# Folding the even columns of a 1024-point transform a third time, both ways, with the spectra kept by column mod 4

## The chip, the cores and the metric

The kernel runs on one core of one Trainium2 chip. The metric is the device time of one execution in microseconds (us); lower is better. Before the change it was 1444.42 us, the median of 3 runs (1443.12 to 1444.52). In this kernel TensorE does the 7562 matmuls (1394.8 us busy) and writes them to the memory PSUM; VectorE (674.9 us) and ScalarE (420.0 us) do most of the rest, among it the evictions, the copies out of PSUM. The granted clock is the share of TensorE's full speed that the profile records. The profile's span is some 2 us shorter than the device time of the same execution (1438.6 against 1440.49 us in before).

## The reference

A gated mix of two branches over x (2048 x 1024), forward and backward. Branch A is a 2-D real FFT, a product with a complex weight and the inverse FFT; branch B is a two-layer MLP with squared ReLU. Cut to what matters:

```python
def _A_ref(x, w_r, w_i):                       # B, S, D = 1, 2048, 1024
    X = jnp.fft.rfft2(x.astype(jnp.float32), axes=(-2, -1))
    X = X * (w_r + 1j * w_i)
    return jnp.fft.irfft2(X, s=(S, D), axes=(-2, -1)).astype(jnp.bfloat16)

def _B_ref(x, w1, b1, w2, b2):                 # F = 3584
    h = jnp.einsum("bsd,df->bsf", x, w1) + b1
    r = jnp.where(h > 0, h, 0)
    return jnp.einsum("bsf,fd->bsd", r * r, w2) + b2

g = sigmoid((x * gate_w).sum(-1, keepdims=True))
out = g * _A_ref(...) + (1 - g) * _B_ref(...)
_out, _vjp = jax.vjp(_f, A_x, A_w_r, A_w_i, B_w1, B_b1, B_w2, B_b2, gate_w)
_grads = _vjp(grad_out)                        # nine outputs in all
```

## The kernel before

The 2-D transform is done twice in parallel (T = 0 for x, T = 1 for the output gradient). In the first stage each of 2 x 16 row tiles goes through `one_s1`. VectorE folds the 1024 columns: `uv` is the sum and difference of the two halves (sum: even columns of the transform, difference: odd), `f` folds each once more about its middle. TensorE then does a small transform along the rows (`pk`) and the **column stage** (`pu`): eight matmuls of 2305 columns in all, 1281 of them for the even columns. P = 128, Q = 256, H = 512, D = 1024.

```python
    def one_s1(fb, cf, T, i, xt, kmat):
        uv = fb.tile([P, 2, H], FDT, name="uv", tag="uv", bufs=2)
        V(out=uv[:, 0, :], in0=xt[:, 0:H], in1=xt[:, H:D], op=ALU.add)
        V(out=uv[:, 1, :], in0=xt[:, 0:H], in1=xt[:, H:D], op=ALU.subtract)
        f = fb.tile([P, 4, Q], FDT, name="f", tag="f", bufs=2)
        a0, a1 = uv[:, :, 1:Q], uv[:, :, H - 1 : Q : -1]
        V(out=f[:, 0:2, 1:Q], in0=a0, in1=a1, op=ALU.add)
        V(out=f[:, 2:4, 1:Q], in0=a0, in1=a1, op=ALU.subtract)
        # (cut: two copies of single elements)
        pk = fps.tile([P, 8, P], FP32, name="pk", tag="ps2", bufs=2)
        fl = f[:].rearrange("p a b -> p (a b)")
        for b in range(8):
            mm(pk[:, b, :], lhsT=fl[:, b * P : (b + 1) * P], rhs=kmat, start=True, stop=True)
        ft = fb.tile([P, 8, P], FDT, name="ft", tag="ft", bufs=2)
        nc.scalar.copy(out=ft[:], in_=pk[:])
        pu = fps.tile([P, 2, H], FP32, name="pu", tag="ps2", bufs=2)
        column_stage(FWD, pu, ft, cf)
        u = fb.tile([P, H, 2], FDT, name="u", tag="u", bufs=2)
        nc.any.tensor_copy(out=u[:].rearrange("p j b -> p b j"), in_=pu[:])
        st(out=z_scr[T][:].rearrange("c (p i) l -> i (c p) l", i=S2)[i], in_=u[:].rearrange("p j b -> p (j b)"))

    FWD = (    # block of ft, PSUM bank, first column, columns, 1 = start + 2 = stop
        (4, 0, 0, H, 1), (0, 0, 0, Q + 1, 0), (1, 0, 0, Q + 1, 0), (5, 0, Q + 1, Q - 1, 2),
        (6, 1, 0, Q, 1), (7, 1, 0, Q, 2), (2, 1, Q, Q, 1), (3, 1, Q, Q, 2),
    )
    INV = (
        (2, 0, 0, H, 1), (0, 0, 0, Q + 1, 0), (1, 0, 0, Q + 1, 0), (3, 0, Q + 1, Q - 1, 2),
        (4, 1, 0, Q, 1), (5, 1, 0, Q, 2), (6, 1, Q, Q, 1), (7, 1, Q, Q, 2),
    )

    def column_stage(table, pu, ft, mat):
        o = 0
        for (b, bank, lo, n, f_) in table:
            mm(
                pu[:, bank, lo : lo + n], lhsT=ft[:, b, :], rhs=mat[:, o : o + n],
                start=bool(f_ & 1), stop=bool(f_ & 2), skip_group_check=True,
            )
            o += n
```

The first stage shares TensorE with the MLP's forward and first backward matmuls (`ph`, `pd`). The middle stage reads the spectra back, transforms along the rows (`px`, evicted as `x`), multiplies by the weights and goes back (`pv`); it runs beside the weight gradients (`pw`, evicted as `wo`). The inverse mirrors the first stage: `pki`, `rt`, a column stage `pui`, an eviction `e`, and folds on VectorE. Parts of the three:

```python
        # spectrum(), the eviction of the row transform; j in 0, 1
            (nc.scalar.copy if j == 0 else nc.vector.tensor_copy)(out=x[:, j, :, 0:H], in_=px[:])

        # fft_out(), one tile
                for b in range(8):
                    par, q4 = divmod(b, 4)
                    mm(pk[:, b, :], lhsT=r[:, q4 * P : (q4 + 1) * P, par], rhs=ki[:], start=True, stop=True)
                rt = fb.tile([P, 8, P], FDT, name="rt", tag="rt", bufs=2)
                nc.scalar.copy(out=rt[:], in_=pk[:])
                pu = fps.tile([P, 2, H], FP32, name="pui", tag="ps2", bufs=2)
                column_stage(INV, pu, rt, ci)
                e = fb.tile([P, 2, H], FDT, name="e", tag="e", bufs=2)
                nc.scalar.copy(out=e[:], in_=pu[:])
                tt = fb.tile([P, 2, 2, Q], FDT, name="tt", tag="tt", bufs=2)
                V(out=tt[:, 0].rearrange("p a b -> p (a b)"), in0=e[:, 0, :], in1=e[:, 1, :], op=ALU.add)
                V(out=tt[:, 1].rearrange("p a b -> p (a b)"), in0=e[:, 0, :], in1=e[:, 1, :], op=ALU.subtract)

        # mlp_grads(), the weight gradients, one block
                    wo = wb.tile([P, D], BF16, name="wo2", tag="wo2", bufs=2)
                    for hf in range(NH):
                        pw = mps.tile([P, H], FP32, name="pw", tag="pw", bufs=2)
                        # (cut: 16 matmuls)
                        last = nc.scalar.copy(out=wo[:, hf * H : (hf + 1) * H], in_=pw[:])
                    # (cut: wo is stored)
```

The opening transposes x and the scaled gradient `dbn` on TensorE (`pt`) and evicts them as `xT` (ScalarE) and `dbT` (VectorE). The order in which these streams are interleaved is written out:

```python
            for i in range(i0, i0 + 4):        # in rows()
                go = f1.tile([P, D], BF16, name="go", tag="go", bufs=4)
                ld(out=go[:], in_=go_perm[i])
                nc.vector.tensor_scalar(out=dbn[:, i, :], in0=go[:], scalar1=omg[:, i : i + 1], scalar2=None, op0=ALU.mult)
                turned(dbT, dbn[:, i, :], i, nc.vector.tensor_copy)

    row_gen, units, first = rows(), mlp_in(), first_stage()
    next(row_gen)
    for i0 in range(0, NT, 4):
        next(units), next(units)
        next(row_gen)
        next(units), next(units)
        next(row_gen, None)
    n = 0
    mixed = spread(units, first, 0.4)          # 0.4 tiles of first for each unit
    while n < 82:
        next(mixed)
        n += 1
    for _ in first:
        pass
```

## Time and profile before

| | before |
|---|---|
| device time, median of 3 runs | 1444.42 us |
| profiled execution | 1440.49 us, span 1438.6 us, mean granted clock 0.995 |
| opening: to the start of the last dbT copy | 88.5 us |
| forward stage: from there to the last dhT eviction | 439.3 us |
| middle stage: from there to the 83rd wo eviction | 355.9 us |
| inverse stage: from there to the first gxo eviction | 357.7 us |
| tail | 197.2 us |

The marks in the table are the starts of single instructions in the trace. What the change also touches are these evictions, from the groups with shapes kept apart (line, engine, operation, out<-in, shapes, count, then busy us and mean ns of one, then idle time before them):

```profile
L251 ACT CAST u<-pu 128x1024 f16<-128x1024 f32 x32 | 41.7, 1304 | 36.8 <-PE pu L267 36.8
...
L306 ACT CAST x<-px 128x1024 f16<-128x1024 f32 x16 | 16.2, 1014 | 5.9 <-PE px L305 5.9
...
L306 DVE CAST x<-px 128x1024 f16<-128x1024 f32 x16 | 19.6, 1224 | 111.5 <-PE px L305 111.5
```

The same 1024 elements take ScalarE 1304 ns into `u`, whose 16-bit elements were written at a step of two, and 1014 ns into `x`, written in runs.

### The profile page before, as it was taken

The numbers are of one execution on the slowest core, as the hardware profiler recorded it, in microseconds if no ns is written. First come the engines' busy times: TensorE is split into PE (matmuls) and PEld (weight loads), VectorE is DVE, ScalarE is ACT, GpSimd is POOL, SyncE is SP. The second block draws the span as 40 slices with busy tenths as digits, with TensorE's granted clock in tenths as the row PEclk, the third lists the DMA queues.
The fourth block names the chain that finished last, engine by engine and source line by source line (L and its number), as shares of the span: only waits on it lengthen the run. The fifth ranks groups of instructions, "written<-read, shape, count | busy, mean of one in ns | idle before, by whom it ended". The sixth has DMA issues, their size and how long they took to land. (4 is left out here: it accounts for less than half of the span.)

```text
span 1438.6 us, 19451 instructions
## 1 busy us (share of the span) xinstructions
PE 1394.8 (97%) x7562; PEld 674.0 (47%) x7562; DVE 674.9 (47%) x1303; ACT 420.0 (29%) x590; POOL 299.3 (21%) x483
## 2 busy tenths in 40 slices
PE   6689999999999999999999999999999999999997
PEld 4455555555554444444444444445554444444443
DVE  2564554455444466445554534113566555652222
ACT  4245555555553322222232222334322100000000
POOL 0012222222223333333442122111110000000000
PEclk9899999999999999999999999999999999999999
DMA  7476766666669967998977678777557647563530
GB/s 234 128 235 205 218 193 204 223 216 205 191 183 255 257 200 201 187 229 189 220 146 187 143 132 188 221 205 231 194 198 228 210 147 221 177 187 96 146 95 22
DMA packets 220214, 271.57 MB, mean 189 GB/s; under 512 B 16077, under 2 KB 153307, under 8 KB 220123
## 3 DMA queue, kind: packets, MB, share of 16 engines
q1 hardware_dynamic: 184122, 151.80, 39.9%
q0 software_dynamic: 36000, 118.54, 27.9%
q8 instruction: 59, 0.97, 0.3%
q14 instruction: 33, 0.26, 0.1%
HBM read 151.77 MB, written 118.51 MB: 188 GB/s over the span
## 5 line engine op out<-in xcount | busy, mean ns | idle before, releaser
L583 PE MATMUL ph<-xT,w1g 128*128 128x512 bf16 x896 | 218.6, 382 | 1.4 <-ACT xT L493 0.9
L591 PE MATMUL pd<-dbT,w2T 128*128 128x512 bf16 x896 | 215.3, 383 | 1.6 <-DVE dbT L493 1.6
L692 PE MATMUL pw<-grp,res 128*128 128x512 bf16 x896 | 209.6, 387 | 0.0
L675 PE MATMUL pw<-dbn,grp 128*128 128x512 bf16 x896 | 198.0, 379 | 1.5 <-DVE row L639 1.5
L753 PE MATMUL acc<-w,hblk 128*128 128x512 bf16 x896 | 198.6, 379 | 0.0
L794 PE MATMUL accg<-w1Tr,hblk 128*128 128x512 bf16 x896 | 193.5, 379 | 0.0
L591 PEld LDWEIGHTS <-w2T 128*128 128x128 bf16 x896 | 87.4, 99 | 109.1 <-issue 5.1
L585 ACT ACTIVATE rT<-ph,b1col 128x512 bf16<-128x512 f32 x112 | 77.0, 688 | 207.9 <-PE ph L583 159.7
L794 PEld LDWEIGHTS <-hblk 128*128 128x128 bf16 x896 | 87.7, 98 | 105.7
L675 PEld LDWEIGHTS <-grp 128*128 128x128 bf16 x896 | 87.1, 98 | 105.8 <-issue 2.4
L692 PEld LDWEIGHTS <-res 128*128 128x128 bf16 x896 | 85.0, 96 | 109.0
L753 PEld LDWEIGHTS <-hblk 128*128 128x128 bf16 x896 | 87.0, 98 | 98.6
L583 PEld LDWEIGHTS <-w1g 128*128 128x128 bf16 x896 | 85.3, 98 | 86.6 <-issue 4.5
L592 DVE SCALAR_TENSOR_TENSOR dhT<-pd,rT 128x512 bf16<-128x512 f32 x112 | 75.3, 673 | 104.5 <-PE pd L591 60.9
L604 DVE STREAM_TRANSPOSE stg<-h2T 128x512 int32<-128x512 int32 x56 | 39.8, 711 | 130.2 <-ACT h2T L586 130.2
L679 ACT CAST wo<-pw 128x512 bf16<-128x512 f32 x56 | 32.8, 586 | 165.7 <-PE pw L675 152.3
L697 ACT CAST wo<-pw 128x512 bf16<-128x512 f32 x56 | 32.9, 587 | 142.0 <-PE pw L692 132.2
L687 POOL DMA_DIRECT2D out_dram<-wo x112 | 56.3, 516 | 81.9 <-ACT wo L679 61.4
L795 DVE TENSOR_TENSOR gxo<-accg,g 128x512 bf16<-128x512 f32 x32 | 22.1, 691 | 107.6 <-PE accg L794 107.4
L306 DVE CAST x<-px 128x1024 f16<-128x1024 f32 x16 | 19.6, 1224 | 111.5 <-PE px L305 111.5
L461 DVE TENSOR_TENSOR tt<-e 128x512 f16<-128x512 f16 x32 | 13.6, 425 | 124.2 <-ACT e L459 123.5
L586 ACT ACTIVATE h2T<-rT 128x512 bf16<-128x512 bf16 x112 | 70.5, 629 | 3.4
(169 smaller groups left out, 1488.6 us busy)
## 6 DMA issues: line engine op xcount, KB each, us to landing
h_scr<-stg POOLq DMA_DIRECT2D x28, 512.0 KB, 6.1
dh_scr<-stg POOLq DMA_DIRECT2D x28, 512.0 KB, 7.4
h2T_scr<-h2T POOLq DMA_DIRECT2D x28, 512.0 KB, 4.9
dhT_scr<-dhT POOLq DMA_DIRECT2D x28, 512.0 KB, 6.6
grp<-h_scr SPq DMA_DIRECT2D x112, 128.0 KB, 5.3
grp<-dh_scr SPq DMA_DIRECT2D x112, 128.0 KB, 4.6
hblk<-h2T_scr SPq DMA_DIRECT2D x8, 1792.0 KB, 9.1
hblk<-dhT_scr SPq DMA_DIRECT2D x8, 1792.0 KB, 8.9
```

The lines of the kernel that those rows point to most:

```text
L583: mm(ph[:], lhsT=w1g[:, dc, fs], rhs=xT[:, dc, ss], start=(dc == 0), stop=(dc == DC - 1))
L585: nc.scalar.activation(rT[:], ph[:], ACT.Relu, bias=b1col[:, fc : fc + 1])
L586: nc.scalar.activation(h2T[:, ss], rT[:], ACT.Square)
L591: mm(pd[:], lhsT=w2T[f2][:, ec, :], rhs=dbT[:, ec, ss], start=(ec == 0), stop=(ec == DC - 1))
L592: STT(out=dhT[:, ss], in0=pd[:], scalar=2.0, in1=rT[:], op0=ALU.mult, op1=ALU.mult, accum_out=gb1part[:, fc, sb : sb + 1],)
L604: nc.vector.transpose(out=stg[k_, sb][:, :, f2, :], in_=src[:, cols2].bitcast(I32).rearrange("p (b i) -> p b i", i=32),)
L675: mm(pw[:], lhsT=cur[:, t // 2, 2 * fb_ * P + t % 2 : 2 * (fb_ + 1) * P : 2], rhs=dbn[:, t, hf * H : (hf + 1) * H], start=(t == 0), stop=( ...
L687: st(out=dst[q], in_=wo[32 * q : 32 * (q + 1), :])
L692: mm(pw[:], lhsT=xr[t][:, d_ * P : (d_ + 1) * P], rhs=cur[:, t // 2, t % 2 :: 2], start=(t == 0), stop=(t == NT - 1),)
L697: nc.scalar.copy(out=wo[:].rearrange("p (q a j) -> p a q j", q=4, j=32), in_=pw[:].rearrange("p (a q j) -> p a q j", q=4, j=32),)
L753: mm(acc[:], lhsT=cur[:, fc, t2::2], rhs=w2[:, fc, cs], start=(fc == 0), stop=(fc == FC - 1))
L794: mm(acc[:], lhsT=cur[:, fc, t2::2], rhs=w1T[:, fc, cs], start=(fc == 0), stop=(fc == FC - 1))
```

## The change

The intent: the part of the signal that belongs to the even columns is folded a third time, so that columns 0 mod 4 and 2 mod 4 are computed apart, each from half as many inputs. The even part of the column stage then takes 256 + 129 + 128 + 128 columns on TensorE in place of 512 + 257 + 257 + 255. VectorE pays with more folds (of `f` forward, into `ev` on the way back). The spectra come out grouped by column mod 4, lie so in DRAM, and are put in order as they leave PSUM in the middle stage. The core of the diff:

```diff
-        f = fb.tile([P, 4, Q], FDT, name="f", tag="f", bufs=2)
+        f = fb.tile([P, 6, Q], FDT, name="f", tag="f", bufs=2)
 (cut)
+        b0, b1 = f[:, 0:3:2, 1:P], f[:, 0:3:2, Q - 1 : P : -1]
+        V(out=f[:, 4:6, 1:P], in0=b0, in1=b1, op=ALU.add)
+        V(out=f[:, 4:6, P + 1 : Q], in0=b0, in1=b1, op=ALU.subtract)
+        V(out=f[:, 4, 0:1], in0=uv[:, 0, 0:1], in1=uv[:, 0, Q : Q + 1], op=ALU.add)
+        V(out=f[:, 4, P : P + 1], in0=uv[:, 0, 0:1], in1=uv[:, 0, Q : Q + 1], op=ALU.subtract)
+        nc.scalar.copy(out=f[:, 5, P::-P], in_=f[:, 0:3:2, P])
 (cut)
-        for b in range(8):
-            mm(pk[:, b, :], lhsT=fl[:, b * P : (b + 1) * P], rhs=kmat, start=True, stop=True)
+        for b, (row, o) in enumerate(((5, P), (4, 0), (4, P), (5, 0), (3, 0), (3, P), (1, 0), (1, P))):
+            mm(pk[:, b, :], lhsT=f[:, row, o : o + P], rhs=kmat, start=True, stop=True)
 (cut)
-        u = fb.tile([P, H, 2], FDT, name="u", tag="u", bufs=2)
-        nc.any.tensor_copy(out=u[:].rearrange("p j b -> p b j"), in_=pu[:])
+        u = fb.tile([P, D], FDT, name="u", tag="u", bufs=2)
+        nc.scalar.copy(
+            out=u[:].rearrange("p (h b r) -> p b h r", h=2, b=2), in_=pu[:].rearrange("p b (h r) -> p b h r", h=2)
+        )
 
     FWD = (
-        (4, 0, 0, H, 1), (0, 0, 0, Q + 1, 0), (1, 0, 0, Q + 1, 0), (5, 0, Q + 1, Q - 1, 2),
-        (6, 1, 0, Q, 1), (7, 1, 0, Q, 2), (2, 1, Q, Q, 1), (3, 1, Q, Q, 2),
+        (0, 0, 2 * P, 0, 1), (0, 0, P + 1, 0, 2), (0, 2 * P, P, 0, 3), (0, 3 * P, P, 0, 3),
+        (1, 0, 2 * P, P, 1), (1, 0, 2 * P, P, 2), (1, P, 2 * P, P, 1), (1, P, 2 * P, P, 2),
     )
+    INV = FWD[:4] + ((1, 0, Q, 0, 1), (1, 0, Q, 0, 2), (1, Q, Q, 0, 1), (1, Q, Q, 0, 2))
 (cut: pm in the middle stage takes the new layout)
-            (nc.scalar.copy if j == 0 else nc.vector.tensor_copy)(out=x[:, j, :, 0:H], in_=px[:])
+            (nc.scalar.copy if j == 0 else nc.vector.tensor_copy)(
+                out=x[:, j, :, 0:H].rearrange("p c (i g) -> p c i g", g=4), in_=px[:].rearrange("p c (g i) -> p c i g", g=4)
+            )
 (cut)
-                for b in range(8):
-                    par, q4 = divmod(b, 4)
-                    mm(pk[:, b, :], lhsT=r[:, q4 * P : (q4 + 1) * P, par], rhs=ki[:], start=True, stop=True)
+                rf = r[:].rearrange("p j b -> p (j b)")
+                for b, (im, l_) in enumerate(((1, 0), (0, 0), (0, 2), (1, 2), (0, 1), (0, 3), (1, 1), (1, 3))):
+                    mm(pk[:, b, :], lhsT=rf[:, im * H + l_ : (im + 1) * H : 4], rhs=ki[:], start=True, stop=True)
 (cut)
+                ev = fb.tile([P, 2, Q], FDT, name="ev", tag="ev", bufs=2)
+                A, B = (e[:, 0, o : o + Q].rearrange("p (c d) -> p c d", c=2) for o in (0, Q))
+                V(out=ev[:, :, 0:P], in0=A, in1=B, op=ALU.add)
+                evf = ev[:].rearrange("p c d -> p (c d)")
+                V(out=evf[:, Q:P:-1], in0=A[:, 0, :], in1=B[:, 0, :], op=ALU.subtract)
+                V(out=evf[:, 2 * Q - 1 : Q + P : -1], in0=B[:, 1, 1:], in1=A[:, 1, 1:], op=ALU.subtract)
+                nc.vector.tensor_copy(out=ev[:, :, P : P + 1], in_=e[:, 0, P::Q].rearrange("p (c o) -> p c o", o=1))
-                V(out=tt[:, 0].rearrange("p a b -> p (a b)"), in0=e[:, 0, :], in1=e[:, 1, :], op=ALU.add)
-                V(out=tt[:, 1].rearrange("p a b -> p (a b)"), in0=e[:, 0, :], in1=e[:, 1, :], op=ALU.subtract)
+                V(out=tt[:, 0].rearrange("p a b -> p (a b)"), in0=evf, in1=e[:, 1, :], op=ALU.add)
+                V(out=tt[:, 1].rearrange("p a b -> p (a b)"), in0=evf, in1=e[:, 1, :], op=ALU.subtract)
```

The constant matrices `cf` and `ci` shrink to match (1665 columns in place of 2305), and the real-valued columns are picked at another step.

More of the change, by code (lines that the diff above doesn't have):

```diff
@@ L64, in build_consts @@
     w = lambda l, d: tp * ((l[None, :] * d[:, None]) % D) / D
-    le, lo = np.arange(0, D // 2 + 1, 2), np.arange(1, D // 2, 2)
-    lei = le[1:-1]
+    l4, l42 = np.arange(0, D // 2 + 1, 4), np.arange(2, D // 2, 4)
+    lo = np.concatenate([np.arange(1, D // 2, 4), np.arange(3, D // 2, 4)])
     d0, d1 = np.arange(P), np.arange(P, 2 * P)
-    dz = d0.copy()
-    dz[0] = Q
-    even = np.zeros((P, 2 * Q))
-    even[:, Q + 1 :] = -np.sin(w(lei, d0))
-    even[0, : Q + 1] = np.cos(w(le, np.array([Q])))[0]
+    dz, dh = d0.copy(), d0.copy()
+    dz[0], dh[0] = Q, P
+    blk_n = np.concatenate([np.zeros((P, P + 1)), -np.sin(w(l4[1:-1], d0))], axis=1)
+    blk_n[0, : P + 1] = np.cos(w(l4, np.array([P])))[0]
     parts = [
-        even,
-        np.cos(w(le, d0)), np.cos(w(le, d1)), -np.sin(w(lei, d1)),
+        blk_n, np.cos(w(l4, d0)), np.cos(w(l42, d0)), -np.sin(w(l42, dh)),
         np.cos(w(lo, d0)), np.cos(w(lo, d1)), -np.sin(w(lo, dz)), -np.sin(w(lo, d1)),
@@ L78, in build_consts @@
     c["cf"] = np.concatenate(parts, axis=1).astype(FDT_NP)
-    de, ds = np.arange(Q + 1), np.arange(1, Q)
+    v = lambda l, d: tp * ((l[:, None] * d[None, :]) % D) / D
+    cof = lambda l: np.where((l == 0) | (l == 2 * Q), 1.0, 2.0)[:, None]
     dq = np.arange(Q)
@@ L83, in build_consts @@
     dzq[0] = Q
-    l0e, l1e = np.arange(0, Q, 2), np.arange(Q, 2 * Q, 2)
-    l0o, l1o = np.arange(1, Q, 2), np.arange(Q + 1, 2 * Q, 2)
-    v = lambda l, d: tp * ((l[:, None] * d[None, :]) % D) / D
-    cof = lambda l: np.where((l == 0) | (l == 2 * Q), 1.0, 2.0)[:, None]
-    ev = np.zeros((P, 2 * Q))
-    ev[1:, Q + 1 :] = -2.0 * np.sin(v(l0e[1:], ds))
-    ev[0, : Q + 1] = np.cos(np.pi * de)
+    m4, m42 = np.arange(0, D // 2, 4), np.arange(2, D // 2, 4)
+    m1, m3 = np.arange(1, D // 2, 4), np.arange(3, D // 2, 4)
+    da = np.arange(P + 1)
+    ev = np.concatenate([np.zeros((P, P + 1)), -2.0 * np.sin(v(m4, da[1:-1]))], axis=1)
+    ev[0] = 0.0
+    ev[0, : P + 1] = np.cos(np.pi * da)
     parts = [
-        ev,
-        cof(l0e) * np.cos(v(l0e, de)), cof(l1e) * np.cos(v(l1e, de)), -2.0 * np.sin(v(l1e, ds)),
-        2.0 * np.cos(v(l0o, dq)), 2.0 * np.cos(v(l1o, dq)), -2.0 * np.sin(v(l0o, dzq)), -2.0 * np.sin(v(l1o, dzq)),
+        ev, cof(m4) * np.cos(v(m4, da)), 2.0 * np.cos(v(m42, d0)), -2.0 * np.sin(v(m42, dh)),
+        2.0 * np.cos(v(m1, dq)), 2.0 * np.cos(v(m3, dq)), -2.0 * np.sin(v(m1, dzq)), -2.0 * np.sin(v(m3, dzq)),
     ]
@@ L239, in one_s1 @@
         V(out=f[:, 2:4, 1:Q], in0=a0, in1=a1, op=ALU.subtract)
-        nc.scalar.copy(out=f[:, 0::3, 0:1], in_=uv[:, :, 0:1])
-        nc.scalar.copy(out=f[:, 2:0:-1, 0:1], in_=uv[:, :, Q : Q + 1])
+        nc.scalar.copy(out=f[:, 3, 0:1], in_=uv[:, 1, 0:1])
+        nc.scalar.copy(out=f[:, 1, 0:1], in_=uv[:, 1, Q : Q + 1])
+        b0, b1 = f[:, 0:3:2, 1:P], f[:, 0:3:2, Q - 1 : P : -1]
[4 more added lines that the diff above has]
+        nc.scalar.copy(out=f[:, 5, P::-P], in_=f[:, 0:3:2, P])
         pk = fps.tile([P, 8, P], FP32, name="pk", tag="ps2", bufs=2)
-        fl = f[:].rearrange("p a b -> p (a b)")
-        for b in range(8):
-            mm(pk[:, b, :], lhsT=fl[:, b * P : (b + 1) * P], rhs=kmat, start=True, stop=True)
+        for b, (row, o) in enumerate(((5, P), (4, 0), (4, P), (5, 0), (3, 0), (3, P), (1, 0), (1, P))):
+            mm(pk[:, b, :], lhsT=f[:, row, o : o + P], rhs=kmat, start=True, stop=True)
         ft = fb.tile([P, 8, P], FDT, name="ft", tag="ft", bufs=2)
@@ L249, in one_s1 @@
         column_stage(FWD, pu, ft, cf)
-        u = fb.tile([P, H, 2], FDT, name="u", tag="u", bufs=2)
-        nc.any.tensor_copy(out=u[:].rearrange("p j b -> p b j"), in_=pu[:])
-        st(out=z_scr[T][:].rearrange("c (p i) l -> i (c p) l", i=S2)[i], in_=u[:].rearrange("p j b -> p (j b)"))
+        u = fb.tile([P, D], FDT, name="u", tag="u", bufs=2)
+        nc.scalar.copy(
+            out=u[:].rearrange("p (h b r) -> p b h r", h=2, b=2), in_=pu[:].rearrange("p b (h r) -> p b h r", h=2)
+        )
+        st(out=z_scr[T][:].rearrange("c (p i) l -> i (c p) l", i=S2)[i], in_=u[:])
     FWD = (
-        (4, 0, 0, H, 1), (0, 0, 0, Q + 1, 0), (1, 0, 0, Q + 1, 0), (5, 0, Q + 1, Q - 1, 2),
-        (6, 1, 0, Q, 1), (7, 1, 0, Q, 2), (2, 1, Q, Q, 1), (3, 1, Q, Q, 2),
-    )
-    INV = (
-        (2, 0, 0, H, 1), (0, 0, 0, Q + 1, 0), (1, 0, 0, Q + 1, 0), (3, 0, Q + 1, Q - 1, 2),
-        (4, 1, 0, Q, 1), (5, 1, 0, Q, 2), (6, 1, Q, Q, 1), (7, 1, Q, Q, 2),
-    )
+        (0, 0, 2 * P, 0, 1), (0, 0, P + 1, 0, 2), (0, 2 * P, P, 0, 3), (0, 3 * P, P, 0, 3),
+        (1, 0, 2 * P, P, 1), (1, 0, 2 * P, P, 2), (1, P, 2 * P, P, 1), (1, P, 2 * P, P, 2),
+    )
+    INV = FWD[:4] + ((1, 0, Q, 0, 1), (1, 0, Q, 0, 2), (1, Q, Q, 0, 1), (1, Q, Q, 0, 2))
     def column_stage(table, pu, ft, mat):
         o = 0
-        for (b, bank, lo, n, f_) in table:
+        for b, (bank, lo, n, skip, f_) in enumerate(table):
+            out = pu[:, bank, lo : lo + n]
+            if skip:
+                out = pu[:, bank, :].rearrange("p (h c i) -> p c h i", h=2, c=2)[:, lo // P]
             mm(
-                pu[:, bank, lo : lo + n], lhsT=ft[:, b, :], rhs=mat[:, o : o + n],
+                out, lhsT=ft[:, b, :], rhs=mat[:, o : o + n],
                 start=bool(f_ & 1), stop=bool(f_ & 2), skip_group_check=True,
@@ L284, in pair_mats, with zg @@
         return t_
+    def zg(ap):
+        return ap.rearrange("p (g c i) -> p c g i", g=4, c=2)
     def spectrum(fb, T, m, z, mats):
         if m:
-            pm = fb.tile([P, 4, H], FDT, name="pm", tag="pm")
-            R = z[:, 0].rearrange("p (a l) -> p a l", a=2)
-            I = z[:, 1].rearrange("p (a l) -> p a l", a=2)[:, ::-1, :]
-            V(out=pm[:, 2:0:-1, :], in0=R, in1=I, op=ALU.add)
-            V(out=pm[:, 0::3, :], in0=R, in1=I, op=ALU.subtract)
-            main = [(pm[:, 0, :], pm[:, 1, :]), (pm[:, 2, :], pm[:, 3, :])]
+            pm = fb.tile([P, 4, 4, P], FDT, name="pm", tag="pm")
+            R, I = zg(z[:, 0]), zg(z[:, 1])[:, ::-1]
+            V(out=pm[:, 2:0:-1], in0=R, in1=I, op=ALU.add)
+            V(out=pm[:, 0::3], in0=R, in1=I, op=ALU.subtract)
+            main = [(pm[:, 0], pm[:, 1]), (pm[:, 2], pm[:, 3])]
         else:
-            main = [(z[:, j, 0:H], z[:, j, H:D]) for j in range(2)]
+            main = [(zg(z[:, j])[:, 0], zg(z[:, j])[:, 1]) for j in range(2)]
         x = fb.tile([P, 2, 2, LW], FDT, name=f"x{T}", tag=f"x{T}")
@@ L311, in real_columns @@
         ed = fb.tile([P, 2, 2, 2, 2], FDT, name="ed", tag="ed", bufs=2)
-        zc = z[:].rearrange("p t c l -> p c t l")[:, :, :, 0::H]
+        zc = z[:].rearrange("p t c l -> p c t l")[:, :, :, 0 : P + 1 : P]
         G = nc.gpsimd
```

## The prediction

> **What bounds the kernel now.** I read the page first (busy times, then the slices), then the groups of instructions with shapes kept apart, then the list of waits of TensorE, then the timeline in the middle of the forward stage and in the first 90 us. The page:
>
> ```profile
> PE 1394.8 (97%) x7562; PEld 674.0 (47%) x7562; DVE 674.9 (47%) x1303; ACT 420.0 (29%) x590; POOL 299.3 (21%) x483
> ...
> PE   6689999999999999999999999999999999999997
> ...
> PEclk9899999999999999999999999999999999999999
> ```
>
> TensorE works nearly all the span at full granted clock, no other engine is above half, and only the first three slices (about 100 us) are loose. The waits of TensorE say the same: they sum to about 34 us, and nearly all of it is in the opening, where the transposes of x and of the scaled gradient wait for VectorE, ScalarE and the first load.
>
> ```profile
> engine line waited for: us in total, times, longest us
> PE pt L492 <- DVE dbn L521: 11.6, 7, 2.2
> PE pt L492 <- DMA xt<-in_A_x_dram: 4.7, 1, 4.7
> ...
> PE pu L267 <- ACT ft L247: 1.8, 1, 1.8
> PE px L302 <- ACT x L306: 1.7, 1, 1.7
> ```
>
> So after 100 us the time is a sum over TensorE's instruction stream: a column streamed less is time saved, unless a new wait takes its place. The column stage that the change shrinks is in these groups (line, engine, operation, tiles, shape, count, then busy us and mean ns):
>
> ```profile
> L267 PE MATMUL pu<-cf,ft 128*128 128x256 f16 x128 | 19.7, 273 | 0.0
> ...
> L267 PE MATMUL pu<-cf,ft 128*128 128x512 f16 x32 | 12.5, 389 | 2.5 <-ACT ft L247 1.8
> ...
> L267 PE MATMUL pu<-cf,ft 128*128 128x257 f16 x64 | 12.4, 275 | 0.0
> ...
> L267 PE MATMUL pu<-cf,ft 128*128 128x255 f16 x32 | 8.7, 273 | 0.0
> ```
>
> The mean of one (273 to 389 ns) is latency of pipelined matmuls, not what each adds. What each adds is read from the starts in the timeline of TensorE (start, us, engine, line, what):
>
> ```profile
> 312.05 0.61 PE L556 MATMUL ptw<-identb,w1g 128*128 128x128 bf16 x8
> 312.50 0.61 PE L245 MATMUL pk<-kg,f 128*128 128x128 f16 x8
> 312.95 1.24 PE L583 MATMUL ph<-xT,w1g 128*128 128x512 bf16 x5
> 314.21 1.17 PE L267 MATMUL pu<-cf,ft 128*128 128x512 f16 x8
> 315.23 0.81 PE L583 MATMUL ph<-xT,w1g 128*128 128x512 bf16 x3
> ```
>
> Eight 128-column matmuls, each with its own weights, take 0.45 us from start to start, 56 ns each; the eight of one column stage, 2305 columns, take 315.23 - 314.21 = 1.02 us. By shape, over all 64 column stages, the start-to-start medians are 226 ns (512 columns), 112 (257 and 255) and 112.5 (256). The five ph matmuls need 5 x 0.216 = 1.08 us but take 1.26: about 0.18 us of hidden wait for the eviction ft (1.01 us) before every column stage. I expect that to stay.
>
> [...] the 56 ns pairs show that a 128-column load hides beside a 128-column matmul in this kernel.[...] The inverse weights now step by 4 elements, 8 bytes[...]; the trace of before has only step 2 (same 56 ns per pair), so nothing there shows step 4.[...] the spectrum's eviction now reads PSUM at a step of 128 elements, and no row of before does such a thing.[...] in the trace 512 elements take 425 ns and 1024 take 684, that is 0.51 ns per further element and 166 ns fixed[...].
>
> **The change part by part.** TensorE, each way, per tile: before 512 + 257 + 257 + 255 + 4 x 256 = 2305 columns in eight matmuls; after 256 + 129 + 128 + 128 + 4 x 256 = 1665, again eight.[...] With the medians above: before 226 + 112 + 112 + 112 + 4 x 112.5 = 1012 ns; after 112.5 + 56.5 + 56 + 56 + 450 = 731 ns. 281 ns less, 32 tiles forward and 32 back: 64 x 0.281 = **18.0 us** off TensorE.[...] Most of it lies in the saturated stretch, so it counts in full there.
>
> VectorE, forward: two tensor_tensor of 254 elements, 166 + 128 = 295 ns each, and two of one element, about 155 ns each (the row of such in before has 153): 0.90 us per tile, 29 us in all. Inverse: one of 256 elements (296 ns), two of about 127 (230 each), one small copy (170): 0.93 us per tile, 30 us. VectorE goes from 675 to about 733 us, still half idle. In the forward stage its row of f and uv operations is 1.7 us, followed by 1.8 to 2.7 us of idle before the next eviction, so 0.9 us more fits in.
>
> ScalarE: one more short copy per forward tile (0.2 us, 6.5 in all), against the eviction u, which wrote every second 16-bit element in 1304 ns and now writes runs of 256; I take 1012 ns as for ft, 32 x 0.29 = 9.3 us less. Net about -3 us, off the path.
>
> Spectrum: the pre-sums, transforms and stores keep their sizes; only the layout moves. The evictions x (16 on ScalarE at 1014 ns, 16 on VectorE at 1224) read PSUM with a step; if this doubles them, +16 and +20 us on engines with slack. DRAM traffic is unchanged but for the constants, 1665 columns in place of 2305.
>
> The opening is what gives something back. The order of the built programs shows that, ahead of the long alternation of ph and pd, the kernel before does two whole column stages and two and a half pk groups between the last transposes of the gradient, while VectorE is the limit there; the changed one does one of each, since its f needs more VectorE work. One column stage (0.73 us) and one and a half pk groups (0.67 us) move from partly idle time into the full stretch, and 0.2 to 0.3 us of VectorE work stands ahead of the last dbT: **about 1.6 us lost**. Otherwise the order of TensorE's stream is nearly the same (groups shift by 2 to 8 matmuls in the inverse).
>
> Sum: 1444.4 - 18.0 + 1.6 = **1428.0 us**, 1.1% faster.
>
> **Rivals.** (1) *The weight loads with a step of 4 become exposed.* Against: step 2 costs nothing[...]. For:[...] that a load's own duration is 98 ns. If each pki pair went from 56 to 98 ns: 256 x 42 = 10.8 us back, 1439 us. One chance in eight or so. (2) *A wait of TensorE for the evictions of ph and pd.* They have two PSUM buffers between them. Measuring in the trace from the end of each pd eviction to the start of the next pd group, the margin is 1.0 us in the median but 0.1 us in the worst twentieth, and for ph 0.3 us at worst. The added copy of f on ScalarE waits for VectorE's sums and usually stands ahead of u and the next rT; if it slips by 0.3 us per tile, up to 32 x 0.3 = 10 us come back, 1438 us.[...] Against: the shorter u gives 0.29 us back just there, and VectorE's idle time is placed before the eviction. I expect 0 to 2 us. (3) *Stepped PSUM reads in the spectrum hold the two shared PSUM buffers.* Before, px waited once, 1.7 us. Between one px group and the next lie 16 matmuls (3.5 us) against about 1.2 us of eviction, so even a doubling costs 0 to 3 us: 1428 to 1431. (4) *VectorE or DMA becomes the bound.* Against: 51% and about 70% busy; not counted. (5) *More gain than counted:*[...] if the new layout of the constants loses that, another 1 us or so.
>
> **Range and chances.** The gain is an arithmetic sum on a saturated engine, so its centre is firm; the losses are one-sided. Rival 5 and a smaller loss in the opening give 1424 as the low end; part of rivals 1 to 3 gives 1437 as the high end. For "faster by over 2%" the time would have to fall below 1415.5, a gain of 29 us where the whole column stage holds 65: I see no source, 0.02. For "slower by over 2%" two rivals together would have to cost over 45 us: 0.01. Within 2%: 0.97.
>
> **What would show it.** Right: the eight matmuls of a column stage take about 0.73 us from start to start, TensorE's busy time falls by about as much as the span, the pki pairs stay at 56 ns, no wait of pd or ph for dhT or rT appears after 100 us, VectorE is near 733 us, u near 1010 ns, and the long ph and pd alternation begins at about 90 us as before but with more still to do. Wrong: pki starts more than 60 ns apart (rival 1); ph or pd groups with waits on VectorE or ScalarE in the forward stage (rival 2); x evictions above 1.5 us with px waiting (rival 3). The prediction itself fails if the forward stage, 90 to 430 us, shortens by much less than its share of about 9 us.

1444.4 - 18.0 + 1.6 = 1428.0 us, the 18.0 from start-to-start medians of the trace (the 56.5 ns for 129 columns is an estimate beside the 56 ns measured for 128), the 1.6 from the order of the instructions and the same starts. VectorE's 166 ns fixed and 0.51 ns per further element are worked out from the trace (425 ns for 512 elements in L234 and L461, 684 for 1024 in L293). Rival 1 rests on the load's record of 98 ns alone. In rival 5, "that" is what a matmul of the column stage takes beyond the dense rate; the trace shows it for 512 columns alone, 226 ns against the 216 of `ph`.

## The result and the profile after

Ratios are those over the fast runs of both kernels from the same rounds, so not quite the ratios of the medians quoted; "less" and "by the ratio" mean that the ratio's distance from 1 is taken of the time of before.

The changed kernel took **1428.82 us** (median of 4 runs, 1422.72 to 1429.50) against 1443.77 before: ratio 0.989, 95% interval 0.986 to 0.9921, which is 15.8 us less. The profiled execution took 1429.31 us, with a span of 1427.5 and a mean granted clock of 0.987.

The page of the kernel after, busy time of the engines and then the granted clock in 40 slices:

```profile
PE 1372.0 (96%) x7419; PEld 668.2 (47%) x7562; DVE 709.5 (50%) x1559; ACT 417.1 (29%) x622; POOL 299.0 (21%) x483
...
PEclk8899999999999999999999999999999999999999
```

The trace lacks 143 of the 7562 matmul records (the page has 7419 beside 7562 weight loads), so TensorE's busy time can't be set against the 1394.8 of before, and I use starts and stages in its place. VectorE gained 34.6 us, ScalarE lost 2.9. Of the clock only the first slice has changed, 8 where before had 9; slices of 36 us are too coarse for what the experiments found.

The column stage on TensorE after (groups, shapes apart):

```profile
L273 PE MATMUL pu<-cf,ft 128*128 128x256 f16 x160 | 28.6, 276 | 0.7
...
L463 PE MATMUL pki<-ki,r 128*128 128x128 f16 x256 | 19.5, 219 | 0.1
...
L273 PE MATMUL pu<-cf,ft 128*128 128x128 f16 x64 | 9.0, 221 | 0.0
...
L273 PE MATMUL pu<-cf,ft 128*128 128x129 f16 x32 | 7.0, 220 | 0.0
```

The 512-column one is gone, and so are the 257s and 255s: per tile five of 256 columns, one of 129 and two of 128. The starts in the timeline, for one of them:

```profile
426.99 0.91 PE L273 MATMUL pu<-cf,ft 128*128 128x256 f16 x8
427.74 0.81 PE L600 MATMUL ph<-xT,w1g 128*128 128x512 bf16 x3
```

By starts, one column stage takes 0.746 us in the median (where no record is missing) and took 1.0125. In order, the medians of its eight matmuls are 119 to 120 ns for the first (256 columns), 57 (129), 61 and 59 (128), and 112 to 113 for the four others of 256. The inverse's `pki` matmuls, whose weights are now read at a step of four elements, follow each other every 56 ns, as before, though the record of one weight load has grown from 98 to 113 ns.

ScalarE and VectorE after (the same view):

```profile
L255 ACT CAST u<-pu 128x1024 f16<-128x1024 f32 x32 | 32.4, 1011 | 17.9 <-PE pu L273 17.9
...
L314 ACT CAST x<-px 128x1024 f16<-128x1024 f32 x16 | 16.2, 1013 | 6.3 <-PE px L313 6.3
...
L314 DVE CAST x<-px 128x1024 f16<-128x1024 f32 x16 | 19.6, 1224 | 113.5 <-PE px L313 113.5
```

Writing `u` in runs took 1011 ns, 293 less than before. The two `x` evictions, which now read PSUM at a step of 128 elements, cost what they cost before: 1013 against 1014 and 1224 against 1224.

The waits of TensorE after:

```profile
PE pt L509 <- DVE dbn L538: 13.4, 8, 2.2
...
PE pd L608 <- DVE dbT L510: 2.5, 4, 0.9
PE px L310 <- ACT x L314: 2.3, 1, 2.3
```

Set beside the prediction's list: `pt` for `dbn` 11.6 then and 13.4 now, `pd` for `dbT` 1.6 and 2.5, the one wait of `px` 1.7 and 2.3. No new kind of wait over 1 us has appeared; these three grew by 3.3 us together, the wait of `pu` for `ft` (1.8 us) is gone, and all waits of TensorE sum to 37.6 us where they summed to 33.4.

By stage the two profiled executions compare so (us):

| stage | before | after | difference | predicted |
|---|---|---|---|---|
| opening | 88.5 | 89.1 | +0.6 | +0.2 to 0.3 |
| forward | 439.3 | 433.6 | -5.7 | about -9, +1.3 to 1.4 |
| middle | 355.9 | 358.2 | +2.3 | 0 to 3 at worst |
| inverse | 357.7 | 349.4 | -8.3 | -9.0 |
| tail | 197.2 | 197.2 | 0.0 | 0 |
| span | 1438.6 | 1427.5 | -11.1 | -16.4 |

Two things stand out. The span fell by 11.1 us and the timed runs by 15.8. The profiled execution of before was a lucky one (1440.49 us, against a median of 1444.42), and that of after one of its three slower ones (at a clock of 0.987; its fastest run, 1422.72 us, had 0.990). And the inverse stage gave what was expected, but the forward stage 3 us less than its share. The experiments are about that shortfall.

### The profile page after: what moved, and what is told of

Read it like the earlier page. It is cut to its first block, busy times and chain, and to the rows that moved or that the text cites. A ratio compares the mean times of both kernels' runs of the same rounds, so it can differ in the third digit from the quotient of the medians.

```text
span 1427.5 us, 19521 instructions
## 1 busy us (share of the span) xinstructions
PE 1372.0 (96%) x7419; PEld 668.2 (47%) x7562; DVE 709.5 (50%) x1559; ACT 417.1 (29%) x622; POOL 299.0 (21%) x483
## 5 line engine op out<-in xcount | busy, mean ns | idle before, releaser
L600 PE MATMUL ph<-xT,w1g 128*128 128x512 bf16 x866 | 215.1, 382 | 3.0 <-ACT xT L510 1.4
L608 PEld LDWEIGHTS <-w2T 128*128 128x128 bf16 x896 | 88.6, 99 | 109.8 <-issue 9.2
L314 DVE CAST x<-px 128x1024 f16<-128x1024 f32 x16 | 19.6, 1224 | 113.5 <-PE px L313 113.5
L704 POOL DMA_DIRECT2D out_dram<-wo x112 | 56.3, 516 | 83.7 <-ACT wo L696 59.6
L718 POOL DMA_DIRECT2D out_dram<-wo x56 | 30.7, 548 | 151.9 <-ACT wo L714 147.0
```

The source lines that it names most:

```text
L600: mm(ph[:], lhsT=w1g[:, dc, fs], rhs=xT[:, dc, ss], start=(dc == 0), stop=(dc == DC - 1))
L608: mm(pd[:], lhsT=w2T[f2][:, ec, :], rhs=dbT[:, ec, ss], start=(ec == 0), stop=(ec == DC - 1))
L704: st(out=dst[q], in_=wo[32 * q : 32 * (q + 1), :])
```

## The experiments

The theory of the prediction: columns saved are time saved, less a debt of order in the opening. The rivals: the column saving itself is smaller than counted; the added folds of VectorE delay TensorE; or something in the opening other than the order of instructions. e1 to e4 went to one chip, e5 to e8 another, e9 and e10 a third.

### e1_cut: the columns alone

On the kernel before, only the tables change: as many columns as the changed kernel streams, nothing else moved. Its spectra are wrong (two outputs off by a relative error of 1.26).

```diff
     FWD = (
-        (4, 0, 0, H, 1), (0, 0, 0, Q + 1, 0), (1, 0, 0, Q + 1, 0), (5, 0, Q + 1, Q - 1, 2),
+        (4, 0, 0, 2 * P, 1), (0, 0, 0, P + 1, 2), (1, 0, 2 * P, P, 3), (5, 0, 3 * P, P, 3),
     INV = (
-        (2, 0, 0, H, 1), (0, 0, 0, Q + 1, 0), (1, 0, 0, Q + 1, 0), (3, 0, Q + 1, Q - 1, 2),
+        (2, 0, 0, 2 * P, 1), (0, 0, 0, P + 1, 2), (1, 0, 2 * P, P, 3), (3, 0, 3 * P, P, 3),
```

> The kernel before with only the matmuls of the column stage narrowed to the widths of the change (256, 129, 128, 128 in place of 512, 257, 257, 255), everything else as before; wrong result on purpose. Theory: TensorE's columns are the whole gain, so this shows the full 18.0 us, 1443.8 - 18.0 = 1426, and is 1 to 4 us faster than the changed kernel, which has a poorer opening. Rival A (the added VectorE work or ScalarE's wait for it costs something in every forward tile): this is over 5 us faster than the changed kernel. Rival B (columns are partly hidden behind the waits for the evictions): the gain stays below 14 us, 1430 or more.

Measured: 1423.52 us (4 runs) against 1441.24 before (9 runs); ratio 0.9879 (0.9866 to 0.9893), 17.5 us less. By stage: forward 431.3 (8.0 less), inverse 349.3 (8.4 less), middle 355.9 (the same). So the columns alone are worth 16.4 us in the two stages and 16.7 us of span. This is 64 x 0.26, and by starts 64 x (1.0125 - 0.746) = 17.1: slightly below the 18.0 predicted. By the ratios it is 1.7 us more than the whole change gives, within the 1 to 4 of the theory.

### e2_pad: everything but the columns

On the kernel after, each column stage streams the 640 saved columns again, as two matmuls whose results are overwritten. The outputs are correct.

```diff
     def column_stage(table, pu, ft, mat):
+        mm(pu[:, 0, :], lhsT=ft[:, 0, :], rhs=mat[:, 0:H], start=True, stop=True, skip_group_check=True)
+        mm(pu[:, 1, 0:P], lhsT=ft[:, 1, :], rhs=mat[:, 0:P], start=True, stop=True, skip_group_check=True)
         o = 0
```

> The changed kernel with 640 columns put back into each column stage (one matmul of 512 and one of 128 columns that the real ones overwrite; right result). TensorE then streams as many columns as before, so what differs from before is all that the change adds elsewhere. Theory: only the opening costs, 1.5 to 4 us: 1445 to 1448. Rival A: over 5 us, 1449 or more. Rival B (columns partly hidden): within 1 us of 1435 to 1440.

Measured: 1444.56 us, ratio 1.0023 (1.0011 to 1.0036) to before: 3.3 us slower. The stages put it in the forward one, 442.1 against 439.3; the inverse is level (358.2 against 357.7), and so are middle (356.2) and opening (88.7). Of the 3.3 us some 0.4 are the padding's own: by starts its ten matmuls take 1.018 to 1.019 us where the eight of before took 1.0125. All that the change adds, folds, layout, stepped reads and order, thus costs some 3 us, and nearly all of it lies in the forward stage or its start.

### e3_forward and e4_inverse: one way each

e3 has the changed first stage and middle and the inverse of before; e4 the other way about (the constants, the tables and the `pki` loop of one or the other kernel). Both are correct.

```diff
 # e3_forward, on after: the inverse of before
-    INV = FWD[:4] + ((1, 0, Q, 0, 1), (1, 0, Q, 0, 2), (1, Q, Q, 0, 1), (1, Q, Q, 0, 2))
+    INV = (
+        (2, 0, 0, H, 0, 1), (0, 0, 0, Q + 1, 0, 0), (1, 0, 0, Q + 1, 0, 0), (3, 0, Q + 1, Q - 1, 0, 2),
+        (4, 1, 0, Q, 0, 1), (5, 1, 0, Q, 0, 2), (6, 1, Q, Q, 0, 1), (7, 1, Q, Q, 0, 2),
+    )
 (cut: ci, the pki loop and tt as before)
 # e4_inverse, on before: the inverse of after
-        (2, 0, 0, H, 1), (0, 0, 0, Q + 1, 0), (1, 0, 0, Q + 1, 0), (3, 0, Q + 1, Q - 1, 2),
+        (0, 0, 0, 2 * P, 1), (1, 0, 0, P + 1, 2), (2, 0, 2 * P, P, 3), (3, 0, 3 * P, P, 3),
 (cut: ci, the pki loop and ev as after)
```

> Only the forward half of the change (and the new order of the spectra), with the inverse of before. Theory: 9.0 us off TensorE, less the 1.5 to 4 us of the opening: 1437 to 1439. Rival A: the forward half gains under 3 us, 1441 or more.

> Only the inverse half, with the forward half and the order of the spectra of before. Theory: the full 9.0 us, nothing lost: 1435. If the weight loads with a step of 4 cost anything: 1438 or more.

Measured: e3 1432.83 us, ratio 0.9934 (0.9921 to 0.9948), 9.5 us less; e4 1430.56 us, ratio 0.9928 (0.9915 to 0.9942), 10.4 us less. The two gains add to 19.9 us, more than the 17.5 of e1 and the 15.8 of the whole change. In both profiled executions the middle stage took 354.0 us, 1.8 less than in before, because the wait of `px` did not occur; that is no part of either half. e3 was expected at 5 to 7.5 us and gained more.

In e3 the forward stage took **431.6 us**, 0.3 above e1, where after took 433.6. But the instructions of e3 stand in the same order as those of after in this stage, with the same folds on VectorE. So neither the order nor the folds can account for the 2.0 us between them. The start of the alternation of `pd` and `ph` shows what does. The timeline of TensorE after (start, us, engine, line, what, idle before):

```profile
88.85 1.06 PE L573 MATMUL ptw<-identb,w2r 128*128 128x128 bf16 x8
...
91.24 2.77 PE L608 MATMUL pd<-dbT,w2T 128*128 128x512 bf16 x6 [0.22 <-issue]
93.80 2.29 PE L600 MATMUL ph<-xT,w1g 128*128 128x512 bf16 x8
```

The same instructions in e3_forward:

```profile
87.12 0.61 PE L571 MATMUL ptw<-identb,w2r 128*128 128x128 bf16 x8
88.74 1.89 PE L606 MATMUL pd<-dbT,w2T 128*128 128x512 bf16 x8 [1.01 <-DVE dbT L508]
90.47 1.89 PE L598 MATMUL ph<-xT,w1g 128*128 128x512 bf16 x8
```

Eight transposes took 1.06 us after and 0.61 in e3; six `pd` matmuls took 2.77 us where eight took 1.89. TensorE works at half speed here, and the view of windows names it. Columns: stretch, its us, busy us (and count) of PE, PEld, DVE, ACT and POOL, then the granted clock, the DMA share and GB/s. After:

```profile
84.00:88.00 4.00, 1.70 (x23) 1.29 (x20) 4.00 (x6) 1.02 (x2) 0.54 (x1) 0.97 0.90 293
88.00:92.00 4.00, 3.23 (x19) 2.28 (x21) 3.75 (x12) 0.48 (x3) 0.00 (x0) 0.50 0.71 226
```

And e3_forward:

```profile
84.00:88.00 4.00, 1.62 (x24) 1.33 (x24) 4.00 (x7) 0.79 (x1) 0.54 (x1) 1.00 0.96 368
88.00:92.00 4.00, 3.26 (x16) 1.48 (x16) 4.00 (x14) 0.49 (x3) 0.34 (x1) 1.00 0.60 187
```

In both, TensorE was busy for only 1.6 to 1.7 of the 4 us before 88, while VectorE was full. After, the clock was then granted at half for 6.8 us, the first of the dense stretch; in e3 it was not. In the seven kernels whose opening is not rewritten, the record of granted clock has, in the stretch from 85 to 102 us:

| at half clock near 88 us | kernels | forward stage, us |
|---|---|---|
| none | before, e1_cut, e3_forward | 439.3, 431.3, 431.6 |
| 3.4 us | e4_inverse | 440.3 |
| 6.8 us | after, e5_again, e2_pad | 433.6, 434.4, 442.1 |

With the new forward stage, 6.8 us at half clock go with a stage longer by 2.0 (after) and 2.8 us (e5_again) than e3's. With the old one, 3.4 us go with 1.0 more (e4 against before).

The debt of order that the prediction counted is there all the same. After the opening, from 91 us on, e3 still has 12 more `pk` and 8 more `pu` matmuls to do than e1: 12 x 0.056 + 0.75 = 1.4 us. What offsets it is a wait that the new order removes. The waits of TensorE's weight loads (engine, line, what for: us in total, times, longest), in before and alike in e1 and e4:

```profile
PEld L591 <- DVE w2T L558: 3.9, 8, 0.5
```

and in e3_forward, alike in after:

```profile
PEld L606 <- DVE w2T L573: 2.1, 9, 0.2
```

Not all of such a wait reaches the matmuls. In before, at each of the eight places, the load waits 0.48 to 0.49 us, and a `ph` group and the `pd` after it start 1.89 us apart instead of 1.73; one of them:

```profile
143.88 1.89 PE L583 MATMUL ph<-xT,w1g 128*128 128x512 bf16 x8
145.77 1.90 PE L591 MATMUL pd<-dbT,w2T 128*128 128x512 bf16 x8
```

A `pd` group waits 0.16 us for its weights `w2T`, whose copy stands behind other VectorE work (before the `pd` of 250.93 us, behind `stg` and `dhT`, from 248.96 to 250.18). In the changed forward order no `pd` starts late (the load's wait of 0.24 us at nine places does not reach it), worth 8 x 0.16 = 1.3 us.

### e5_again and e6_order: the debt of order returned

e5 is the kernel after once more. e6 is after with two more tiles of the first stage drawn into the opening, so that TensorE does about as much there as in the kernel before.

```diff
         next(row_gen)
+        for _ in range({12: 2}.get(i0, 0)):
+            next(first)
         next(units), next(units)
```

> The changed kernel once more, as the control of the three below, to see its spread. Theory: the gain of the columns less the opening, 1424 to 1429 beside a before of 1441 to 1444; ratio 0.988 to 0.991.

> The changed kernel with two forward tiles written ahead of the last round of the opening's transposes; the order built has again two column stages and two pk groups between the last transposes of the gradient, as the kernel before had. Theory: the opening loses 1.5 us by order and up to 2.5 us by the half clock that follows the idle stretch, and both come back: 2 to 4 us faster than the changed kernel of the same call, ratio to before about 0.986 to 0.987. Rival (the loss is elsewhere, in VectorE's additions of the steady stage): no difference over 1 us.

Measured: e5 1426.98 us (6 runs, 1422.6 to 1429.33, clocks 0.986 to 0.992) against 1441.60 (11 runs); ratio 0.9892 (0.9873 to 0.9911), 15.6 us less: the first result again. e6 1425.37 us, ratio 0.9886 (0.9871 to 0.9901), 16.4 us less. The 2 to 4 us expected did not come, and the intervals overlap, so the times do not tell the two apart: inconclusive. e6's forward stage is 431.7 us, 2.7 less than e5's, with 3.4 us at half clock near 88 us instead of 6.8. But its last `dbT` came at 90.2 us, where e5's came at 87.9, so the forward stage ended only 0.4 us sooner (521.9 against 522.3 us). The trace shows why: the added `pk` group and column stage start at 89.95 and 92.12 us, after the last transposes, so they filled none of the idle time before these. The edit restored the amount of work in the opening, and the opening grew.

e5 also shows how far one trace of the same kernel may lie from another. Its middle stage took 356.0 us where the first trace of after had 358.2. In that first trace, the timeline of TensorE shows why (the `px` wait of the list above):

```profile
673.81 1.67 PE L692 MATMUL pw<-dbn,grp 128*128 128x512 bf16 x7
677.81 0.38 PE L310 MATMUL px<-pm,amat 128*128 128x512 f16 x1 [2.33 <-ACT x L314]
...
678.62 0.63 PE L313 MATMUL px<-pm,amat 128*128 128x512 f16 x1
```

and on ScalarE, which is late for another reason:

```profile
676.26 0.58 ACT L696 CAST wo<-pw 128x512 bf16<-128x512 f32 x1 [8.79 <-DMA out_dram<-wo]
676.74 1.02 ACT L314 CAST x<-px 128x1024 f16<-128x1024 f32 x1
```

The eviction `wo` waits 8.79 us, by the profile for a store out of one of its two buffers; the eviction `x`, which follows it in ScalarE's order, waits with it; `px` waits for `x`. After the gap of 2.33 us the clock was granted at half for 3.4 us, which I estimate to cost half of that, 1.7 us; with the 0.7 us by which the gap grew, that is the 2.3 us of the stage. In e5 the gap was 1.77 us and no half clock followed.

### e7_early6 and e8_before_early6: a fuller opening, on both kernels

Two tiles each in the second, third and fourth round of the opening, on after and on before.

```diff
         next(row_gen)
+        for _ in range({4: 2, 8: 2, 12: 2}.get(i0, 0)):
+            next(first)
         next(units), next(units)
```

> The changed kernel with six forward tiles in the opening, two in each of the last three rounds of transposes, where TensorE waits for VectorE and ScalarE. Each tile has 0.45 + 0.73 us of TensorE work; four more tiles than in the version above, at most 4.7 us more, less what the opening grows by VectorE's 2.6 us per tile: 3 to 8 us faster than the changed kernel, 1418 to 1424.

> The same early start of six tiles in the kernel before. If the opening's idle time is a thing of its own, this gains 3 to 7 us as well, ratio about 0.996, and the change is worth about 17 to 18 us between the two early versions (0.988) without the loss in the opening.

Measured: e7 1419.96 us (1415.85 to 1421.76), ratio 0.9844 (0.9825 to 0.9863), 22.5 us less than before and 6.9 less than e5. e8 1434.82 us (1431.96 to 1436.46), ratio 0.9951 (0.9936 to 0.9965), 7.1 us less than before. The fuller opening is thus worth 7 us on either kernel. Its forward stage is 426.4 us in e7 (e5: 434.4) and 432.8 in e8 (before: 439.3), and the last `dbT` comes hardly later (88.6 against 87.9, and 88.5 in both): the moved tiles ran in time in which TensorE had waited for VectorE and ScalarE.

Between the two early versions the change is worth 22.5 - 7.1 = 15.4 us, as between after and before. The expectation was 17 to 18. If the debt of order were all of the shortfall, more than 15.4 us should have come, since six tiles are written into both openings (at the last `dbT`, e7 has 212 `pk` and 216 `pu` matmuls left and e8 208 and 213, some 0.5 us apart); that was not confirmed by the times. In e7's trace 3.4 us at half clock remain near 88 us. In e8's trace the gap before `px` was 2.74 us, again followed by 3.4 us at half clock (middle stage 358.3).

### e9_wo4 and e10_split: two waits taken away

e9 is e7 with four buffers for `wo`, so that its eviction need not wait for a store. e10 is e9 with every second `dbT` copy on ScalarE, since the longest waits of TensorE in the opening are for VectorE.

```diff
-                    wo = wb.tile([P, D], BF16, name="wo2", tag="wo2", bufs=2)
+                    wo = wb.tile([P, D], BF16, name="wo2", tag="wo2", bufs=4)
 (e10 only)
-                turned(dbT, dbn[:, i, :], i, nc.vector.tensor_copy)
+                turned(dbT, dbn[:, i, :], i, nc.scalar.copy if i % 2 else nc.vector.tensor_copy)
```

> The early start of six tiles, and four buffers in place of two for the gradient's output tiles wo. In most traces so far TensorE waits 1.1 to 2.7 us once, some 145 us into the gradient stage, for a px buffer held by ScalarE, which stands behind a wo that waits for its store, and a half-clock window sometimes follows. If that is the chain, this wait goes and the time falls by 1 to 3 us against the early start (ratio to before 0.983 or below, about 1417 to 1419); if the buffer is not the cause the wait of px stays.

> As the one before, and every second copy dbT of the opening moved from VectorE to ScalarE. VectorE's chain of four dbT (1.29 us each) is what the transposes of the gradient wait for; two of four moved shorten each of the four rounds by 1 to 2 us, 4 to 8 us in all: 1411 to 1415, ratio 0.978 to 0.981, which could pass 2%. If ScalarE's own work (xT, rT, ft, u) takes the place, under 2 us.

Measured: e9 1415.37 us (1414.42 to 1417.20) against 1445.19 before (9 runs); ratio 0.9795 (0.9776 to 0.9815), at 2% unclear. Against e7 that is some 7 us by the ratios, across two chips, where 1 to 3 were expected; between the two traces it is 4.3 us, 3.2 of them in the opening. e10 **1407.94 us** (5 runs, 1407.33 to 1410.06), ratio 0.9747 (0.9728 to 0.9767), 7.4 us less than e9, within the 4 to 8 expected. Both are correct.

The wait of `px` in e7, the group of its first matmul:

```profile
L310 PE MATMUL px<-pm,amat 128*128 128x512 f16 x28 | 10.6, 379 | 1.4 <-ACT x L314 1.1
```

and in e9:

```profile
L310 PE MATMUL px<-pm,amat 128*128 128x512 f16 x28 | 10.6, 379 | 0.3
```

The idle time is gone, and the middle stage took 354.0 us in e9 and e10, against 355.3 in e7 and 355.9 in before. This is also what it took in e3 and e4, in which the wait happened not to occur, so with two buffers it was absent in two of ten traces, with four in two of two. e9's last `dbT` came at 85.4 us, 3.2 earlier than e7's, though nothing in the opening had changed. Some 1.3 us of that arise between 58.3 and 60.8 us of e7, in a half-clock stretch (3.4 us from 57.4 on) that e9 does not have there; what did the rest stays open, so I do not count it for the four buffers.

The waits of TensorE in e10:

```profile
PE pt L509 <- DVE dbn L538: 3.9, 3, 2.2
...
PE ptw L573 <- DVE dbT L510: 1.7, 3, 0.7
```

The wait for `dbn` fell from 8.6 us in e7 and e9 to 3.9. The last `dbT` started at 79.7 us in place of e9's 85.4, the forward stage nearly kept its length (425.8 against 426.6), and no half clock was granted near 88 us. All five runs of e10 had a mean clock of 0.996 or 0.997. This is the best version, and beats both kernels.

## Why the prediction was right

**The columns: right, a little large.** The term was 64 x 0.281 = 18.0 us. e1_cut, which saves only the columns, gained 17.5 us by the ratio, and the starts give 64 x 0.2665 = 17.1. The new stage was put at 731 ns and takes 746. Half of the 15 ns is its first matmul: I put in 112.5 ns for its 256 columns, as for the others, and it takes 119 to 120. The other half is the two of 128 columns, 61 and 59 ns in place of 56. The gain that rival 5 hoped for, from the 10 ns by which the 226 of a 512-column matmul here exceed the 216 of `ph`, went the other way.

**The opening: the sum held, one part was missing and one was offset.** The step said 1.6 us lost: 1.4 by order and 0.2 to 0.3 by VectorE work ahead of the last `dbT`. The debt of order is in the records at that size (1.4 us, counted in e3 against e1), but the new order also saves 1.3 us of waits for `w2T`, which I had not looked for among the waits of the weight loads. The 0.2 to 0.3 us cannot be told: the opening took 89.1 us in one trace of after and 87.9 in the other. In its place stands the half clock at the start of the dense stretch. It was in all three traces of the complete new kernel and its padded form (after, e5, e2), at 2.0 to 2.8 us; e3, with the same stream in this stage, escaped it. So it is not a fixed cost of the order. That the idle time before 88 us brings it on is argued, not shown. Over all twelve traces, the last gap of TensorE over 1 us before the dense stretch (not counting a second one of 1.0 us in e3 and e5) was 2.00 to 2.11 us in seven, and six of these were granted half clock next (after, e5, e2, e6, e7, e9), but not e3; it was 1.17 to 1.82 us in four, and one of these was (e4, but not before, e1, e8); e10 had no gap over 1 us and no half clock. The new order lengthens this gap from 1.82 us (1.17 in e1) to 2.1, so the half clock may come with the change more often than without; what decides in one execution is open. In the middle of full streams, single gaps of 2.33 us (after) and 2.74 us (e8) were each followed by 3.4 us at half clock; gaps of 1.59 to 1.99 us (e6, before, e1, e5, e2) were not. Two cases are few. Every stretch at half clock that ended inside the spans of before and after was 3.4, 6.8 or 10.2 us long.

The sign of failure that I named, a forward stage that shortens by much less than 9 us, was thus in part met: 5.7 us in the first trace and 4.9 in e5. The columns gave their share (8.0 us in e1); the half clock took the rest. I also had the stage end at 430 us; by the marks it ends at 527.8.

**The middle stage: not foreseen, and not due to the change.** The prediction allowed 0 to 3 us for stepped PSUM reads. The first trace lost 2.3 us there, but the evictions take the same 1013 and 1224 ns as before. The wait comes from the stores of `wo`. It is in before as well (1.66 us), it varies from run to run (absent in e3 and e4), and in both traces with four buffers it is gone (e9, e10).

**The rivals.** Rival 1, exposed weight loads: wrong, `pki` stays at 56 ns; the load's own record did grow, from 98 to 113 ns, but stays hidden. Rival 2, `pd` and `ph` waiting for evictions: the hidden wait before each column stage, summed over the forward stage, was 5.53 us before and 5.71 after. The prediction expected it to stay, and it did. Rival 3: wrong, as told. Rival 4 stayed off the path.

**VectorE: the sum was too large.** I said about 733 us; the page says 709.5. The durations were nearly right: over all of VectorE's records they sum to 56.0 us more (59 predicted). But records of neighbouring instructions overlap, and the page counts their union: in after the durations sum to 801.3 us where the page has 709.5, in before to 745.4 where it has 674.9. The timeline of VectorE after shows it:

```profile
312.96 0.15 DVE L243 TENSOR_TENSOR f<-uv 128x1 f16<-128x1 f16 x1
313.03 0.15 DVE L244 TENSOR_TENSOR f<-uv 128x1 f16<-128x1 f16 x1
313.10 0.29 DVE L241 TENSOR_TENSOR f<-f 128x254 f16<-128x254 f16 x1
313.30 0.28 DVE L242 TENSOR_TENSOR f<-f 128x254 f16<-128x254 f16 x1
313.50 0.42 DVE L231 TENSOR_TENSOR uv<-src 128x512 f16<-128x512 bf16 x1
```

The four added folds take 313.50 - 312.96 = 0.54 us from start to start, where I counted 0.90 by durations. Over the 256 added instructions the surplus is 56.0 - 34.6 = 21.4 us, 84 ns each; read directly, a record overlaps the next by 82 ns in the median (1140 places in after). ScalarE went down by 2.9 us, as said (about 3), with `u` at 1011 ns.

**The time.** Predicted 1428.0; measured 1428.82 and, a second time, 1426.98. The parts that I had too large (0.9 us of columns, the order offset by waits) and those that I had not seen (half clock) nearly cancel, so that it came within 1 us is luck; the 18 us of columns are not. A margin of some 3 us to either side is the run-to-run spread. In the changed kernel it mostly goes with the granted clock (after and e5: six runs of 1427.3 to 1429.5 us at 0.986 to 0.988, three of 1422.6 to 1423.5 at 0.990, but one of 1426.67 at 0.992); in the kernel before it does not (1442.02 us at 0.988, 1442.76 at 0.994).

## What to carry to other kernels

Where one engine is full, take a saving from start-to-start times in the trace, not from durations of records; here that held for the engine that saves (matmuls of the column stage with records of 273 to 389 ns started 112 to 226 ns apart) and for the one that pays (four folds with records of 0.87 us in all took 0.54). After such a change look first at the places where the saturated engine was not full before: here the opening and one wait for a store, untouched by the change, held more (21 us, between e5 and e10, by their ratios to before) than the change itself (16 us). Before explaining 2 or 3 us between two single traces, compare their granted clocks in narrow windows and take a second trace of the same kernel.
